# A long convolution by a two-stage Fourier transform: K's buffer as pairs of channels, and the product written into it

## The chip, the cores and the metric

The kernel runs on one core of one Trainium2 chip. The metric is the device time of one execution in microseconds. Before the change it is 544.58 us, the median of three runs (544.21 to 545.67). The engines are named as in the profile: PE is TensorE (PEld its weight loads, PEq its sequencer), DVE is VectorE, ACT is ScalarE, POOL is GpSimd, SP is SyncE, which issues nearly all DMAs.

## The reference

All data are float32. There are 2048 positions and 640 channels.

```
xn = layernorm(u)                                   # over the 640 channels
A  = -exp(log_A_real) + 1j*A_imag                   # 640 x 128 states
C  = (C_real + 1j*C_imag) * dt[:, None]
K  = 2 * einsum("dn,dnl->dl", C, exp(A*dt*l)).real  # one kernel of 2048 taps per channel
s  = irfft(rfft(xn, 4096) * rfft(K, 4096))[:2048] + xn * D_skip
g  = silu(xn + y)         # y: a gated feed-forward (640 -> 1728 -> 640) for the 8 positions
                          # with the highest xn @ w_r, zero elsewhere
out = u + s * g
```

So each channel is convolved with its own kernel of 2048 taps, and the gate is the silu of the normalized input, with 8 of the 2048 positions put through a feed-forward first.

## The kernel before, in words

**Tiling.** The 640 channels are seen as 4 blocks of 160 (the index d), the 2048 positions as 32 x 64. The large tile `g_all` is [128, 64, 2, 160]: partitions are (block, coarse position), then the fine position b, a real or imaginary plane, and 160 channel columns g, of which 32 neighbours make a batch. Seen as `gm` it is [128, 128 columns m, 160 channels g]. There are 5 batches (lines 25 to 29), each of 32 columns g, worked in groups of four: 40 groups.

**The steps of a batch.**

- K is generated for each group of four (`kernel`, line 819): POOL builds magnitudes by doubling (L829 to L836, tiles ma and mb), TensorE makes angles (L845), ACT takes their sine (L854), DVE multiplies (L856 to L867, tiles ta and tb), TensorE contracts over the states (L878), ACT copies the result into a buffer kb (L884; a ring of 5), and D_skip is added to its first tap (L885).
- First stage of the transform (`stage1`, line 897): K from kb gives a PSUM tile, which is copied into `fk` (L889 to L892), [128, 32 channels, 128 columns], channel by channel. For the input it is L906, copied back into `gm` (L908).
- Second stage (`transform`, line 913), for each kp from 0 to 7: a table `mt` of 4 x 128 columns is loaded; `dft` (L928) multiplies it with four columns of K (moving operand `k2`, from `fk`) and with four columns of the input (moving operand `u2`, from `gm`). In both, column 32 d + 4 kp + e belongs to kp. The moving operand runs over d and over the 32 channels.
- The complex product. K's result is copied to `kr` (L975), halves are swapped by DMAs into `ki` and `kr` (L976, L977), DVE forms `xa` (L989) and the main product (L992), which is written into `gm` over the input's columns (`u4`). `xa` has its halves swapped by DMAs into `xb` (L1007), and POOL adds it to `gm` (L1009; recorded as L392, since `tt` is a helper).
- In the last batch (QUICK) the input's transform is done early and copied into `gm` (L940 to L945), and for seven of the kp K's transform is made twice with its halves exchanged, in half-width matmuls (L958), so that no swap of K is needed.
- The inverse, four channels at a time (L1012 to L1022): the stationary operand is `gm[:, :, h + e]`, one channel's 128 columns with a step of 160 words; the moving operand is a constant. The result is copied into the same channels of `g_all` (L1020; recorded as L389, since `copy` is a helper), reading PSUM straight through and writing with a step of 160 words.
- The tail (line 1026) does the last inverse stage and the gate for the first three batches (L1047, L1054) and for the last two (L1118, L1124), adds the input and stores the output.

**What orders the work.** Every step is a task with the engines it can run on, a cost in us, what it reads and writes, and slots of rings of buffers. `Plan.order` simulates the engines and takes, on each engine, the ready task with the highest priority: the longest path behind it plus a weight from the table BIAS for its kind. PT is what a change of ACT's table set counts in that. The instructions are then issued in that order on every engine and on SP's queue. The task names that matter here are `s1k` and `s1ke` (first stage of K and its copy), `s2k`, `s2q`, `s2u` (second stages), `x1`, `xa`, `xadd` (the product), `inv` and `inve`.

**Who holds fk.** The first stage of the next batch's K may write `fk` as soon as the eight second-stage tasks of K of the batch before have read it (L889, key `fkfree` of the batch; L1010). The inverse of that batch reads `gm` and doesn't concern `fk`. Before the batches, `fk` serves as scratch (line 1146).

The lines that the steps of the prediction name:

```
copy(e, fk[:, q:q + 4].rearrange("p g m -> p (g m)"), p.t)                     # L891
k2 = fk[:, :ng].rearrange("p g (d k) -> p k d g", k=32)                        # L917
T.matmul(p.t[:, n * e:n * e + n], m.t[:, e], f[:, 4 * kp + e], start=True, stop=True)   # L930
T.matmul(p.t[:, 128 * e:128 * e + 128], gm[:, :, h + e], c[:, C_D:C_D + 128], start=True, stop=True)   # L1017
```

Of the kernel before, what the change touches and what calls it, by code (L numbers as in the profile page):

```python
# [21 lines left out]

L, D, N, FF, NSEL = 2048, 640, 128, 1728, 8
# [9 lines left out]
STEP = 7.3  # L33
# [5 lines left out]
PT = 45.962  # L39
BIAS = {  # L40
    "": -1188.3, "K": 3796.4, "arg": 1046.0, "evk": -8566.5, "exp": 2553.4, "ff": 15766.9, "inv": -8312.6,
    "inve": -8085.8, "kb": 907.3, "kswap": -0.0, "ln": 1669.4, "load": 11542.5, "mags": -1264.8, "mt": 4371.9,
# [23 lines left out]
def shape_constants():  # L66
# [25 lines left out]
    m[0, :, :, 1], m[1, :, :, 1] = np.sin(ph), np.cos(ph)  # L92
    l = 64 * a[None] + bm[:, None]
# [240 lines left out]
def kernel(ctx: ExitStack, tc: tile.TileContext, xq, xp, xr, par, ldtp, dsk, wr, wg, wu, wd,  # L334
# [19 lines left out]
    ring("kb", 5, [128, 4, 64], "fft")  # L354
# [14 lines left out]
    fk = k.tile([128, NG, 128], F32, name="fk")  # L369
    fuf = fk.rearrange("p g m -> p (g m)")  # L370
# [303 lines left out]
    def router():  # L674
        p = Slot("f")
        for j in range(5):
# [10 lines left out]
            on("PE", 1.52, mm, ["xn", ("wx", j)], [("rt", j)] + ([p] if j else []), [] if j else [p], mac=.853)  # L687
# [131 lines left out]
    def kernel(gg):  # L819
# [69 lines left out]
        on("PE", .9, lambda: stage1(p.t, lambda e: kb.t[:, e]), [kb, ("fkfree", batch(gg)), "c"], new=[p],  # L889
           kind="s1k", mac=.853)  # L890
        P.add(EVAC, lambda e: copy(e, fk[:, q:q + 4].rearrange("p g m -> p (g m)"), p.t),  # L891
# [21 lines left out]
    def transform(bi):  # L913
# [3 lines left out]
        k2 = fk[:, :ng].rearrange("p g (d k) -> p k d g", k=32)  # L917
        u2 = gm[:, :, g0:g0 + ng].rearrange("p (d k) g -> p k d g", k=32)
        vw = lambda t: t.rearrange("p (k d g) -> p k d g", k=4, d=4)
# [8 lines left out]
        def dft(p, f, m, kp):  # L928
            for e in range(4):
                T.matmul(p.t[:, n * e:n * e + n], m.t[:, e], f[:, 4 * kp + e], start=True, stop=True)  # L930
# [7 lines left out]
        if quick:  # L938

            for kp in range(8):  # L940
                m, pu, u4 = load_m(kp), Slot("f"), u2[:, 4 * kp:4 * kp + 4]
# [4 lines left out]
        for kp in range(8):  # L946
            m, xa = load_m(kp, [("U", bi, q) for q in range(8) if quick]), Slot("xa")
            kdep = [m] + [("fk", 4 * gg - g0) for gg in gs]
            u4 = u2[:, 4 * kp:4 * kp + 4]

            if quick and kp in QTWICE:
                pk = Slot("pr")

                def twice(pk=pk, m=m, kp=kp):
                    for h in range(2):
                        for e in range(4):
                            for half in range(2):
                                T.matmul(pk.t[64 * half:64 * half + 64, 1 - h, n * e:n * e + n],  # L958
                                         m.t[:, e, 64 - 64 * h:128 - 64 * h], k2[:, 4 * kp + e], start=True, stop=True,
                                         tile_position=(0, 64 * half))  # L960

                on("PE", 3.9, twice, kdep, [("S2K", bi, kp)], [pk], kind="s2q", mac=1.707)
# [6 lines left out]
                on("DVE", .6, lambda u4=u4, pk=pk: V.tensor_tensor(u4, u4, vw(pk.t[:, 0, :nn]), op=OP.mult),  # L969
                   [pk], [("X", bi, kp)], kind="x1")  # L970
            else:
                pk, krk, kik, pu = Slot("f"), Slot("kr"), Slot("ki"), Slot("f")
                on("PE", 1.78, lambda pk=pk, m=m, kp=kp: dft(pk, k2, m, kp), kdep, [("S2K", bi, kp)], [pk, krk],
# [8 lines left out]
                if quick:  # L982
# [3 lines left out]
                    on("DVE", .6, lambda u4=u4, krk=krk: V.tensor_tensor(u4, u4, vw(krk.t[:, :nn]), op=OP.mult),  # L986
# [215 lines left out]
```

## Time and profile before

| | us |
|---|---|
| median of three runs | 544.58 |
| the profiled execution | 540.41 |
| its span, first to last instruction | 538.6 |
| from the start to the first second-stage matmul of K | 139.3 |
| first inverse | 219.4 |
| last K product (L878) begins | 416.0 |
| last batch's K transform (L958) begins | 449.4 |

The granted clock of TensorE was 0.993 on average. A float32 matmul shows as two records in the trace, so that a call of `dft` (four matmuls) is eight records. The durations of single TensorE records overlap: the mean ns of one is its latency, and the price in a stream comes from the start and the end of an unbroken run. A group's idle time names what ended it; for an engine that isn't the bottleneck it costs nothing. DMA share is the mean busy share of the core's 16 DMA engines.

### The profile page before, as it was taken

How to read it: one execution, taken by the hardware profiler on the slowest of the kernel's cores; microseconds unless marked ns; L12 is line 12 of the kernel's file. 1: busy time of each engine (PE TensorE's matmuls, PEld its weight loads, DVE VectorE, ACT ScalarE, POOL GpSimd, SP SyncE). 2: the span in 40 equal slices, each digit the busy share in tenths (PEclk: the TensorE clock that was granted, in tenths of full speed). 3: DMA queues.
4: the chain of work that ended last, by engine and by line, in shares of the span. 5: the costliest groups of instructions: out<-in, count | busy, mean ns of one | idle time of the engine just before them, and what ended most of it. 6: DMA issues, size and time to landing. Idle time of an engine off the chain costs nothing.

```text
span 538.6 us, 16912 instructions
## 1 busy us (share of the span) xinstructions
PE 486.8 (90%) x6871; PEld 391.5 (73%) x6871; DVE 381.7 (71%) x801; ACT 291.6 (54%) x437; POOL 304.5 (57%) x706
## 2 busy tenths in 40 slices
PE   1039999999998899999999999999999999999994
PEld 1014977656665568888889878888888998866984
DVE  6999099774579846999877999778834133578245
ACT  2009587677734248955677657866645542332420
POOL 7250459973759586898968998958942900000000
PEclk9999999999998999989999999999999999999999
DMA  8909502544789962246642656115675187798956
GB/s 255 311 1 276 138 28 77 167 135 146 194 205 202 219 163 62 71 99 173 185 114 49 160 129 179 41 35 156 158 219 144 52 214 201 203 261 266 258 162 192
DMA packets 91126, 84.84 MB, mean 158 GB/s; under 512 B 41384, under 2 KB 65640, under 8 KB 91048
## 3 DMA queue, kind: packets, MB, share of 16 engines
q1 hardware_dynamic: 90792, 83.71, 57.2%
q8 instruction: 54, 0.88, 0.7%
q14 instruction: 24, 0.20, 0.1%
q0 software_dynamic: 256, 0.04, 0.0%
HBM read 50.02 MB, written 10.51 MB: 112 GB/s over the span
## 4 chain that ended last, share of the span: by engine, by line
PE 60%; DVE 14%; DMA 12%; POOL 5%; SPq 5%; issue 3%; ACT 1%; DVEq 0%; POOLq 0%; ACTq 0%
PE f L901 13%; PE f L930 11%; PE f L1017 9%; PE pr L845 5%; PE f L878 5%; DMA wflat<-wd 5%; PE f L404 3%; PE f L767 3%; PE f L685 2%; PE f L1047 2%; DMA xb<-xa 2%; PE pr L958 2%; SPq L419 2%; POOL mb L834 2%; DMA g_all<-xq 1%
## 5 line engine op out<-in xcount | busy, mean ns | idle before, releaser
L834 POOL TENSOR_TENSOR mb<-mb,et 128x32 f32<-128x32 f32 (+4 forms) x200 | 107.9, 540 | 0.0
L854 ACT ACTIVATE pr<-pr 128x1024 f32<-128x1024 f32 x80 | 81.2, 1020 | 34.7 <-PE pr L845 32.4
L389 ACT COPY g_all<-f 128x512 f32<-128x512 f32 x65 | 64.3, 1000 | 52.7 <-PE f L1017 35.9
L1017 PE MATMUL f<-c,g_all 128*128 128x128 f32 x320 | 75.1, 383 | 0.0
L1017 PEld LDWEIGHTS f<-c,g_all 128*128 128x128 f32 x320 | 72.6, 311 | 3.0 <-issue 0.9
L836 POOL TENSOR_TENSOR ma<-ma,et 128x16 f32<-128x16 f32 (+4 forms) x200 | 74.6, 373 | 0.0
L858 DVE TENSOR_TENSOR tb<-pr,mb 128x512 f32<-128x512 f32 x80 | 54.5, 681 | 18.6 <-PE f L878 15.3
L930 PE MATMUL f<-fk,mt 128*128 128x128 f32 x264 | 63.1, 398 | 1.2 <-DVE fk L389 1.2
L930 PEld LDWEIGHTS f<-fk,mt 128*128 128x128 f32 x264 | 52.8, 206 | 9.0 <-DVE fk L389 1.4
L856 DVE TENSOR_TENSOR ta<-pr,ma 128x512 f32<-128x512 f32 x80 | 54.3, 682 | 6.8 <-ACT pr L854 3.2
L901 PEld LDWEIGHTS f<-c,g_all 128*64 128x64 f32 x640 | 49.7, 250 | 11.1 <-issue 3.6
L392 POOL TENSOR_TENSOR g_all<-g_all,xb 128x512 f32<-128x512 f32 x32 | 41.1, 1287 | 26.8 <-DMA xb<-xa 11.9
L901 PE MATMUL f<-c,g_all 128*64 128x128 f32 x640 | 55.0, 319 | 0.1
L845 PE MATMUL pr<-pos,st 128*128 128x512 f16 x160 | 48.1, 386 | 2.1 <-DVE sv L440 1.2
L878 PE MATMUL f<-tb,ta 128*32 128x64 f32 x2560 | 47.3, 223 | 0.0
L878 PEld LDWEIGHTS f<-tb,ta 128*32 128x32 f32 x2560 | 40.5, 111 | 9.1 <-issue 5.1
L930 PE MATMUL f<-g_all,mt 128*128 128x128 f32 x320 | 43.9, 284 | 0.9 <-DMA mt<-cm 0.6
L930 PEld LDWEIGHTS f<-g_all,mt 128*128 128x128 f32 x320 | 40.3, 196 | 5.9 <-issue 3.1
L901 PE MATMUL f<-c,kb 128*64 128x128 f32 x640 | 40.5, 276 | 0.0
L901 PEld LDWEIGHTS f<-c,kb 128*64 128x64 f32 x640 | 34.7, 137 | 6.9 <-issue 2.8
L389 DVE COPY g_all<-f 128x512 f32<-128x512 f32 x23 | 24.3, 1057 | 17.2 <-PE f L901 14.5
L1072 POOL MEMSET wflat<- 128x2048 f32 x1 | 1.8, 1808 | 58.3 <-DVE g_all L1054 58.3
(155 smaller groups left out, 807.2 us busy)
## 6 DMA issues: line engine op xcount, KB each, us to landing
mt<-cm SPq DMA_DIRECT2D x48, 256.0 KB
xb<-xa SPq DMA_DIRECT2D x78, 128.0 KB
ki<-kr SPq DMA_DIRECT2D x66, 128.0 KB
g_all<-xq SPq DMA_DIRECT2D x8, 640.0 KB
xg_d<-g_all SPq DMA_DIRECT2D x16, 320.0 KB
wflat<-wg SPq DMA_DIRECT2D x10, 432.0 KB
wflat<-wu SPq DMA_DIRECT2D x10, 432.0 KB
wflat<-wd SPq DMA_DIRECT2D x16, 270.0 KB
```

What stands on the lines that cost most here:

```text
L389: {"ACT": S.copy, "DVE": V.tensor_copy, "POOL": G.tensor_copy}[e](out, in_)
L392: {"DVE": V, "POOL": G}[e].tensor_tensor(out, a, b, op=op)
L834: G.tensor_tensor(b[:, :, :, w:2 * w], b[:, :, :, :w], e[:, q].unsqueeze(2).unsqueeze(3).broadcast_to([128, 16, 2, w]), op=OP.mult)
L836: G.tensor_tensor(a[:, :, w:2 * w], a[:, :, :w], e[:, 6 + q].unsqueeze(2).broadcast_to([128, 16, w]), op=OP.mult)
L845: T.matmul(o.t[:, h], st.t[:, 2 * (gg % 8) + h], pos[:, 512 * f:512 * f + 512], start=True, stop=True)
L854: on("ACT", .96, lambda src=src: S.activation(src.t, src.t, AF.Sin, scale=-TWO_PI), [], [src], table="TS", kind="sin")
L856: on("DVE", .6, lambda i=i, src=src: V.tensor_tensor(half(ta.t[:, i]), side(src, 0), half(ma.t), op=OP.mult), [src, ma] + ([] if i else [t ...
L858: on("DVE", .6, lambda i=i, src=src: V.tensor_tensor(half(tb.t[:, i, :, 0]), side(src, 1)[:, :, :, ::-1], half(mb.t[:, :, 1]), op=OP.mult) ...
L878: T.matmul(o[32 * d4:32 * d4 + 32, dl, :], ta.t[:, i, cc, :], tb.t[:, i, cc].rearrange("p h j -> p (h j)"), start=(i == 0), stop=(i == 1), ...
L901: T.matmul(p[64 * ri:64 * ri + 64, 128 * e:128 * e + 128], src(e), c[:, C_W + 128 * ri:C_W + 128 * ri + 128], start=True, stop=True, tile_ ...
L930: T.matmul(p.t[:, n * e:n * e + n], m.t[:, e], f[:, 4 * kp + e], start=True, stop=True)
L1017: T.matmul(p.t[:, 128 * e:128 * e + 128], gm[:, :, h + e], c[:, C_D:C_D + 128], start=True, stop=True)
```

## The change

`fk` becomes [128, 16 pairs, 128 columns, 2]: the two channels of a pair are neighbours, then the columns, then the pairs. Columns are dealt to kp in another way: column 32 d + 8 i + kp belongs to kp, so that the sixteen columns of one kp have a constant step of 8; the table `cm` has its rows permuted to match. The transforms write their PSUM tile in the order (d, i, channel), in four runs of 32 columns per matmul.

The main product and the addition of `xb` now write into `fk` (`z4`), over those columns of K that this kp's transform has read; `gm` keeps the input's values until the inverse's copy. The inverse takes its stationary operand from `fk`: one channel's 128 columns with a step of two words. Its copy reads PSUM with a step of 128 words and writes four neighbouring words at a time.

The place of four channels in `fk` now becomes free when their inverse has read it, so `fkfree` is kept for each group of four instead of for the batch. The ring kb grows from 5 to 8 buffers. The copy of K into `fk` writes every second word.

The planner's costs of `s2k` and `inv` become 0.95 us and that of `s2q` 2.0, and the router's 2.6, and PT and all weights in BIAS are others, so that the order of issue on every engine can differ.

```
-    ring("kb", 5, [128, 4, 64], "fft")
+    ring("kb", 8, [128, 4, 64], "fft")
...
-    fk = k.tile([128, NG, 128], F32, name="fk")
+    fk = k.tile([128, NG // 2, 128, 2], F32, name="fk")
...
+    m = m[:, :, (np.arange(8)[:, None] + 8 * np.arange(4)).reshape(-1)]
...
-        on("PE", .9, lambda: stage1(p.t, lambda e: kb.t[:, e]), [kb, ("fkfree", batch(gg)), "c"], new=[p],
+        on("PE", .9, lambda: stage1(p.t, lambda e: kb.t[:, e]), [kb, ("fkfree", q), "c"], new=[p],
            kind="s1k", mac=.853)
-        P.add(EVAC, lambda e: copy(e, fk[:, q:q + 4].rearrange("p g m -> p (g m)"), p.t),
+        P.add(EVAC, lambda e: copy(e, fk[:, q // 2:q // 2 + 2].rearrange("p h m r -> p h r m"),
+                                   p.t.rearrange("p (h r m) -> p h r m", h=2, r=2)),
...
+        k2 = fk.rearrange("p h (d i k) r -> p i k d h r", d=4, k=8)
+        u2 = gm[:, :, g0:g0 + ng].rearrange("p (d i k) g -> p i k d g", d=4, k=8)
+        vw = lambda t: t.rearrange("p (x g) -> p x g", x=16)
+        vz = lambda t: t.rearrange("p (x h r) -> p x h r", x=16, r=2)
+        vc = lambda t, e: t.rearrange("p (d i g) -> p i d g", d=4, i=4)[:, e]
+        vu = lambda t: t.rearrange("p x (h r) -> p x h r", r=2)
+        in_u = lambda kp: gm[:, kp::8, g0:g0 + ng]
+        in_z = lambda kp: fk[:, :, kp::8].rearrange("p h x r -> p x h r")
...
-                T.matmul(p.t[:, n * e:n * e + n], m.t[:, e], f[:, 4 * kp + e], start=True, stop=True)
+                T.matmul(vc(p.t[:, :nn], e), m.t[:, e], f[:, e, kp], start=True, stop=True)
...
-                    on("DVE", .6, lambda u4=u4, pu=pu, krk=krk: V.tensor_tensor(
-                        u4, vw(pu.t[:, :nn]), vw(krk.t[:, :nn]), op=OP.mult), [pu, krk], [("X", bi, kp)], kind="x1")
+                    on("DVE", .6, lambda z4=z4, pu=pu, krk=krk: V.tensor_tensor(
+                        z4, vz(pu.t[:, :nn]), vz(krk.t[:, :nn]), op=OP.mult), [pu, krk, ("S2K", bi, kp)], [("X", bi, kp)],
+                       kind="x1")
...
-                     lambda e, u4=u4, xb=xb: tt(e, u4, u4, vw(xb.t[:, :nn]), OP.add), [xb], [("X", bi, kp)], kind="xadd")
-        P.join([("fkfree", bi + 1)], [("S2K", bi, kp) for kp in range(8)])
+                     lambda e, z4=z4, xb=xb: tt(e, z4, z4, vz(xb.t[:, :nn]), OP.add), [xb], [("X", bi, kp)], kind="xadd")
...
-                    T.matmul(p.t[:, 128 * e:128 * e + 128], gm[:, :, h + e], c[:, C_D:C_D + 128], start=True, stop=True)
...
-            P.chain(("i", gg % 8), on("PE", 1.77, inv, [("Xall", bi), "c"], new=[p], kind="inv", mac=.853), 8 * STEP)
-            P.add(EVAC_COL, lambda e, p=p, h=h: copy(
-                e, g_all[:, :, :, h:h + 4].rearrange("p b r g -> p g b r"),
-                p.t.rearrange("p (g b r) -> p g b r", g=4, b=64)), [p], [("y", bi, gg)], kind="inve")
+                    T.matmul(p.t[:, 128 * e:128 * e + 128], fk[:, (q + e) // 2, :, e % 2], c[:, C_D:C_D + 128],
+                             start=True, stop=True)
+
+            P.chain(("i", gg % 8), on("PE", .95, inv, [("Xall", bi), "c"], [("fkfree", h - g0)], [p], kind="inv", mac=.853),
+                    8 * STEP)
+            P.add(EVAC_COL, lambda e, p=p, h=h: copy(e, gm[:, :, h:h + 4], p.t.rearrange("p (g m) -> p m g", g=4)),
+                  [p] + [("U", bi, kp) for kp in range(8)], [("y", bi, gg)], kind="inve")
...
-    P.join([("fkfree", 0)], ["diag", "ones", "m2"] + [("sts", b) for b in range(0, NB, 4)])
+    for q in range(0, NG, 4):
+        P.join([("fkfree", q)], ["diag", "ones", "m2"] + [("sts", b) for b in range(0, NB, 4)])
```

The same change of target is made in the last batch's two forms of the product.

More of the change, by code (lines that the diff above doesn't have):

```diff
@@ L38 @@
 QTWICE = (1, 2, 3, 4, 5, 6, 7)
-PT = 45.962
+PT = 51.488
 BIAS = {
-    "": -1188.3, "K": 3796.4, "arg": 1046.0, "evk": -8566.5, "exp": 2553.4, "ff": 15766.9, "inv": -8312.6,
-    "inve": -8085.8, "kb": 907.3, "kswap": -0.0, "ln": 1669.4, "load": 11542.5, "mags": -1264.8, "mt": 4371.9,
[6 rows of a table removed]
+    "": -182.6, "K": 20620.6, "arg": 3785.6, "evk": -1312.8, "exp": 2366.8, "ff": -119.1, "inv": 21575.7,
+    "inve": 7516.6, "kb": 285.9, "kswap": -6679.6, "ln": -1.4, "load": -1205.7, "mags": 9237.9, "mt": 1730.4,
[5 rows of a table added]
+    307.9, "xadd": 15271.2, "xq": -6876.5, "xswap": -876.9,
 }
@@ L368 @@
     gm = g_all.rearrange("p b r g -> p (b r) g")
-    fk = k.tile([128, NG, 128], F32, name="fk")
-    fuf = fk.rearrange("p g m -> p (g m)")
+    fk = k.tile([128, NG // 2, 128, 2], F32, name="fk")
+    fuf = fk.rearrange("p h m r -> p (h m r)")
     c = k.tile([128, C_END], F32, name="c")
@@ L686, in mm @@
                              start=(j == 0 and i < 4), stop=(j == 4 and i > 27), tile_position=(0, t))
-            on("PE", 1.52, mm, ["xn", ("wx", j)], [("rt", j)] + ([p] if j else []), [] if j else [p], mac=.853)
+            on("PE", 2.6, mm, ["xn", ("wx", j)], [("rt", j)] + ([p] if j else []), [] if j else [p], mac=.853)
         r4 = wflat[:, L:L + 64]
@@ L940, in transform @@
             for kp in range(8):
-                m, pu, u4 = load_m(kp), Slot("f"), u2[:, 4 * kp:4 * kp + 4]
+                m, pu, u4 = load_m(kp), Slot("f"), in_u(kp)
                 P.chain(("u", kp), on("PE", .95, lambda pu=pu, m=m, kp=kp: dft(pu, u2, m, kp), [m] + udep, [("U", bi, kp)],
@@ L948, in transform @@
             kdep = [m] + [("fk", 4 * gg - g0) for gg in gs]
-            u4 = u2[:, 4 * kp:4 * kp + 4]
+            u4, z4 = in_u(kp), in_z(kp)
             if quick and kp in QTWICE:
@@ L957, in twice @@
                             for half in range(2):
-                                T.matmul(pk.t[64 * half:64 * half + 64, 1 - h, n * e:n * e + n],
-                                         m.t[:, e, 64 - 64 * h:128 - 64 * h], k2[:, 4 * kp + e], start=True, stop=True,
+                                T.matmul(vc(pk.t[64 * half:64 * half + 64, 1 - h, :nn], e),
+                                         m.t[:, e, 64 - 64 * h:128 - 64 * h], k2[:, e, kp], start=True, stop=True,
                                          tile_position=(0, 64 * half))
-                on("PE", 3.9, twice, kdep, [("S2K", bi, kp)], [pk], kind="s2q", mac=1.707)
+                on("PE", 2.0, twice, kdep, [("S2K", bi, kp)], [pk], kind="s2q", mac=1.707)
                 on("ACT", .57, lambda pk=pk: S.activation(pk.t[:, 1, :nn], pk.t[:, 1, :nn], AF.Copy,
@@ L968, in transform @@
                    [pk, ("sK", bi, kp), ("X", bi, kp)], new=[xa], kind="xa")
-                on("DVE", .6, lambda u4=u4, pk=pk: V.tensor_tensor(u4, u4, vw(pk.t[:, 0, :nn]), op=OP.mult),
+                on("DVE", .6, lambda u4=u4, z4=z4, pk=pk: V.tensor_tensor(z4, vu(u4), vz(pk.t[:, 0, :nn]), op=OP.mult),
                    [pk], [("X", bi, kp)], kind="x1")
@@ L985, in transform @@
                         vw(xa.t[:, :nn]), u4, vw(kik.t[:, :nn]), op=OP.mult), [kik, ("X", bi, kp)], new=[xa], kind="xa")
-                    on("DVE", .6, lambda u4=u4, krk=krk: V.tensor_tensor(u4, u4, vw(krk.t[:, :nn]), op=OP.mult),
-                       [krk], [("X", bi, kp)], kind="x1")
+                    on("DVE", .6, lambda u4=u4, z4=z4, krk=krk: V.tensor_tensor(z4, vu(u4), vz(krk.t[:, :nn]), op=OP.mult),
+                       [krk, ("S2K", bi, kp)], [("X", bi, kp)], kind="x1")
                 else:
@@ L1002, in transform @@
                 on("PE", .9, turn, [xa, "c"], new=[ps2], kind="xq")
-                on("DVE", .6, lambda u4=u4, ps2=ps2: V.tensor_tensor(u4, u4, vw(ps2.t[:, :nn]), op=OP.add), [ps2],
+                on("DVE", .6, lambda z4=z4, ps2=ps2: V.tensor_tensor(z4, z4, vz(ps2.t[:, :nn]), op=OP.add), [ps2],
                    [("X", bi, kp)], kind="xq")
```

7 lines of the change are left out of this document (2 added, 5 removed), and 11 rows, old and new, of the table BIAS.

## The prediction

> **What bounds the kernel now.** The page comes first: the share of each engine, and the chain of work that ended last.
>
> ```profile
> span 538.6 us, 16912 instructions
> PE 486.8 (90%) x6871; PEld 391.5 (73%) x6871; DVE 381.7 (71%) x801; ACT 291.6 (54%) x437; POOL 304.5 (57%) x706
> PE 60%; DVE 14%; DMA 12%; POOL 5%; SPq 5%; issue 3%; ACT 1%; DVEq 0%; POOLq 0%; ACTq 0%
> ```
>
> TensorE is busy 90% of the span and is 60% of the chain, but DVE, the DMAs and POOL hold 31% of it. A cut in TensorE work is therefore not worth the same everywhere, and the second view is the busy time by stretch (columns: length, then PE, PE weight loads, DVE, ACT and POOL busy with their instruction counts, granted clock, DMA share, GB/s). I cut at 220 us (the first inverse), at 350 (near the end of the dense K generation) and at 449 (the last batch's K transform).
>
> ```profile
> 68.00:220.00 152.00, 145.84 (x2144) 102.11 (x2143) 115.02 (x233) 96.66 (x135) 106.66 (x258) 0.99 0.54 142
> 220.00:350.00 130.00, 126.89 (x1822) 110.35 (x1821) 117.51 (x221) 90.32 (x136) 114.94 (x287) 0.99 0.48 124
> 350.00:449.00 99.00, 98.09 (x1302) 88.56 (x1302) 52.26 (x84) 54.41 (x75) 53.11 (x104) 1.00 0.53 144
> 449.00:538.60 89.60, 80.38 (x1196) 66.29 (x1192) 48.86 (x87) 24.36 (x39) 2.83 (x2) 1.00 0.78 220
> ```
>
> From 68 us on TensorE hardly rests. Yet from 220 to 350 DVE is at 90% and POOL at 88% as well, so there three engines end within 12 us of each other. From 350 to 449 TensorE is alone (99%; DVE and POOL 53 and 54%). From 449 on the DMA engines are at 0.78.
>
> The third view is the groups by shape. It says which TensorE instructions are dear (count, then busy us and the mean ns of one).
>
> ```profile
> L1017 PE MATMUL f<-c,g_all 128*128 128x128 f32 x320 | 75.1, 383 | 0.0
> L1017 PEld LDWEIGHTS f<-c,g_all 128*128 128x128 f32 x320 | 72.6, 311 | 3.0 <-issue 0.9 <-DVE g_all L1003 0.2 <-ACT fk L389 0.2
> L930 PE MATMUL f<-fk,mt 128*128 128x128 f32 x264 | 63.1, 398 | 1.2 <-DVE fk L389 1.2
> L930 PE MATMUL f<-g_all,mt 128*128 128x128 f32 x320 | 43.9, 284 | 0.9 <-DMA mt<-cm 0.6 <-ACT g_all L389 0.3
> L930 PEld LDWEIGHTS f<-g_all,mt 128*128 128x128 f32 x320 | 40.3, 196 | 5.9 <-issue 3.1 <-ACT fk L389 0.9 <-ACT g_all L389 0.4
> L958 PE MATMUL pr<-fk,mt 128*64 128x128 f32 x224 | 29.6, 438 | 1.6 <-DVE g_all L969 1.6
> ```
>
> All rows of L930 and L1017 have one shape, 128 rows by 128 columns in float32. What differs is how the operand lies. In g_all 32 channels lie side by side (L930, 284 ns). In fk the next channel is 128 words on (L930 with fk, 398 ns). The inverse's stationary operand steps over 160 words (L1017: its weight load takes 311 ns against 196). These durations overlap, so the price of one comes from unbroken runs in the timeline of TensorE (start, length, line, count):
>
> ```profile
> 288.63 5.49 PE L930 MATMUL f<-fk,mt 128*128 128x128 f32 x24
> 402.69 4.94 PE L930 MATMUL f<-g_all,mt 128*128 128x128 f32 x40 [0.27 <-DMA mt<-cm]
> 409.56 4.59 PE L901 MATMUL f<-c,kb 128*64 128x128 f32 x80
> 423.63 5.33 PE L1017 MATMUL f<-c,g_all 128*128 128x128 f32 x24
> 460.45 7.65 PE L958 MATMUL pr<-fk,mt 128*64 128x128 f32 x64
> ```
>
> Per record that is 229 ns with fk, 124 ns with g_all, 57 ns for a half-width one with dense operands, 222 ns for the inverse, 120 ns for the half-width one with fk.
>
> **The change, part by part: the cheaper operands.** In the new fk two channels lie side by side and the next pair 256 words on. So K's moving operand comes in runs of two words. I take the dense price for it: 229 - 124 = 105 ns saved on each of 264 records, 27.7 us. The half-width ones (L958) go from 120 to 57 ns: 224 x 63 = 14.1 us. The inverse's stationary operand now steps over two words instead of 160. Again I take the dense price, 222 - 124 = 98 ns on 320 records, 31.4 us. Together 73 us. The bounds are the dense price and today's: no row shows runs of two words or a step of two, so either saving can also be nil; I stand nearer the dense rows, because pairs halve the jumps and a step of 8 bytes lies far nearer to 4 than to 640.
>
> [...]
>
> **Where these savings count.** The records by stretch (PE's count is the first in brackets; tile fk, then line 1017):
>
> ```profile
> 68.00:220.00 152.00, 15.60 (x64) 12.54 (x64) 0.70 (x1) 8.33 (x14) 0.99 0.54 142
> 220.00:350.00 130.00, 30.31 (x128) 25.90 (x128) 2.72 (x4) 7.11 (x12) 0.99 0.48 124
> 350.00:449.00 99.00, 17.17 (x72) 14.37 (x72) 0.00 (x0) 5.22 (x9) 1.00 0.53 144
> 220.00:350.00 130.00, 29.47 (x126) 28.43 (x125) 0.99 0.48 124
> 350.00:449.00 99.00, 30.10 (x128) 28.96 (x128) 1.00 0.53 144
> 449.00:538.60 89.60, 14.92 (x64) 14.37 (x64) 1.00 0.78 220
> ```
>
> - 68 to 220: 64 x 105 = 6.7 us. TensorE is not busy for 6.2 us of the stretch, so others already hold part of it; I count 4.
> - 220 to 350: 128 x 105 + 126 x 98 = 25.8 us. DVE still has its 117.5 us; at 96% busy the stretch would be 122.4 long. I count 8: DVE and POOL are next in line and keep the other 18.
> - 350 to 449: 72 x 105 + 128 x 98 = 20.1 us, and nothing else is near. I count 20.
> - 449 to the end: 14.1 + 64 x 98 = 20.4 us. The same bytes at a DMA share of 0.90 instead of 0.78 need 89.6 x 0.78 / 0.90 = 77.7 us. I count 11.
>
> The sum is 43 us. The profiled execution took 540.4 us, its span 538.6 and 1.8 around it; it lies 4.2 us below the median of the runs, 544.6. So 540.4 - 43 = 497.4 profiled, and 502 as a median.
>
> **The other edits.**
>
> ```profile
> L389 ACT COPY fk<-f 128x512 f32<-128x512 f32 x35 | 20.7, 594 | 6.8 <-PE f L901 6.7
> L389 DVE COPY fk<-f 128x512 f32<-128x512 f32 x5 | 3.4, 684 | 0.1
> L389 DVE COPY g_all<-f 128x512 f32<-128x512 f32 x23 | 24.3, 1057 | 17.2 <-PE f L901 14.5
> L992 DVE TENSOR_TENSOR g_all<-f,kr 128x512 f32<-128x512 f32 x32 | 21.5, 678 | 0.0
> L389 ACT COPY g_all<-f x65: 586/1052/1144, 71.8 to 515.7; 128x512 f32<-128x512 f32 x65
> L392 POOL TENSOR_TENSOR g_all<-g_all,xb 128x512 f32<-128x512 f32 x32 | 41.1, 1287 | 26.8 <-DMA xb<-xa 11.9 <-PE pr L845 6.7 <-DVE tb L867 4.6
> L834 POOL TENSOR_TENSOR mb<-mb,et 128x32 f32<-128x32 f32 x40 | 10.9, 273 | 0.0
> L836 POOL TENSOR_TENSOR ma<-ma,et 128x32 f32<-128x32 f32 x40 | 10.4, 261 | 0.0
> ```
>
> The copy of K into fk (40 of them) now writes every second word: on ACT between 594 ns and the 1052 ns of a copy into columns of g_all. I take 594; at worst it is 40 x 0.46 = 18 us of ACT, which is busy 90 of 130 us in its fullest stretch, and one copy of delay in each of four batches, 2 us. The product's write in pairs (40 on DVE) costs 678 ns as now up to 678 + (1057 - 684) = 1051: nil taken, at worst 24 x 0.37 = 9 us on DVE where it bounds. The inverse's copy reads PSUM with a step of 128 words and writes four words together: between 586 and 1052 + 466 = 1518 ns; I take today's 1052, since one hop replaces another. POOL's addition (1287 ns) over pairs: 32 elements in single words take POOL 273 ns, in pairs 261, so hops are nearly free there; nil taken, twice the time as the upper end. The transforms' output in PSUM goes in four runs of 32 columns instead of one of 128, three jumps per matmul; nil. The bytes of the tables and of the swaps through SP's queue stay.
>
> Added is a wait. The first stage of K for four channels now waits for the inverse of the four channels that held their place, where it waited for the last K transform only. It stands on TensorE's queue; behind it wait the angles and products of the next K groups, and the whole next transform. Eight kb buffers instead of five let K generation run on meanwhile. All queues are issued in another order; the rows can't price that. The four stretches hold 19 us in which TensorE isn't busy, so I allow 10 either way.
>
> **Rivals.** The stages of the loop that the new wait closes, from the first K transform of a batch to its last addition:
>
> ```profile
> 228.66 2.00 PE L930 MATMUL f<-fk,mt 128*128 128x128 f32 x8 [1.24 <-DVE fk L389]
> 281.01 1.29 POOL L392 TENSOR_TENSOR g_all<-g_all,xb 128x512 f32<-128x512 f32 x1 [2.96 <-PE pr L845]
> 343.56 1.27 POOL L392 TENSOR_TENSOR g_all<-g_all,xb 128x512 f32<-128x512 f32 x1
> 355.24 2.00 PE L930 MATMUL f<-fk,mt 128*128 128x128 f32 x8
> 410.27 2.53 POOL L392 TENSOR_TENSOR g_all<-g_all,xb 128x512 f32<-128x512 f32 x2 [0.89 <-DMA xb<-xa]
> 449.40 7.74 PE L958 MATMUL pr<-fk,mt 128*64 128x128 f32 x64
> ```
>
> With 288.63 from above the stages last 53.6, 56.2 and 57.6 us. Today the next one starts 6.3 and 10.4 us after the last addition (36.6 before the last batch, with the tail's work in between), its K already in fk. With the change 64 inverse records (7.9 us), 128 first-stage records (7.3) and a copy (0.6) come between: 15.8.
>
> 1. *The forecast, 502.* Each stage loses its own 64 x 105 = 6.7 us, so 49.1 on average. Started 4 us earlier, the last batch's K transform comes at 224.7 + 3 x (49.1 + 15.8) = 419, 30 us before today's, which agrees with 4 + 8 + 20. Chance 0.50, own range 485 to 518.
> 2. *The loop bounds.* Swaps, additions and DVE, not TensorE, set the stage, and it stays as long. Then the K transforms start at 282.3 + 15.8 = 298.1, + 56.2 + 15.8 = 370.1, + 57.6 + 15.8 = 443.5, which is 5.9 us before today's; with the first stretch's 4 and the tail's 11 that is 21 us: 524. For it: POOL and DVE at 88 and 90%. Against it: TensorE was full in every stage. Chance 0.17.
> 3. *Only the moving operand gains.* A weight load may pay for every word that doesn't lie next to the last, whatever the step; then the inverse stays at 222 ns and its load at 311. By stretch I count 4, 6 (TensorE keeps 12 us more there), 7.6 and 9, so 27 us, 518. Against it: none of the rows has a step below 640 bytes. [...] Chance 0.12.
> 4. *All of it comes through*, the new order filling DVE and POOL evenly: 544.6 - 73 = 472. Against it: the DMAs of the tail. Chance 0.11.
> 5. *Slower: POOL's addition over pairs takes twice its time*, 2.6 us. It lies in the loop eight times a batch: three stages of 10.3 us more against the second rival's 21 us, 31 - 21 = 10: 555. It decides from 21 / 24 = 0.9 us more per addition. Against it: 273 and 261 ns above. Chance 0.05.
> 6. *The pairs do nothing for TensorE.* The loop then holds 14.2 + 7.3 + 0.6 = 22.1 us between stages, and the last K transform starts at 462.5: 13 later, 558. Chance 0.03.
>
> **The numbers.** The likeliest gives 502. Faster by over 0.3% (1.6 us, about what a measurement of this kernel can tell from no change): 0.50 + 0.17 + 0.12 + 0.11 = 0.90. Slower: 0.08. The 0.02 left lies between. A range of 476 to 530 takes in the first three cases and the upper half of the fourth; it leaves out the slower ones.
>
> **What would show it.** Right: the fk transform and the inverse near 280 ns each with a weight load under 200, TensorE's busy sum near 415 us, its share below 90%, DVE above 76%, the last K transform near 419 us. The second rival shows as waits of TensorE for the copy into fk, and stages still 54 to 58 us; the third as L1017's weight load still near 311; the fifth as additions over 2.2 us. The forecast is wrong if TensorE's sum falls by 73 us and the span by less than 20, or if POOL's or DVE's sums grow by over 15 us.

## The result, and the profile after

The changed kernel takes 525.6 us, the median of four runs (521.7 to 528.6), against 545.1 for four runs of the kernel before: a ratio of 0.963, interval 0.956 to 0.971. That is 19.6 us faster, inside the range, and less than half of the 42.6 us that were forecast. The profiled execution took 528.6 us, the slowest of the four; the one before took 540.4, less than any of its four, so that the spans of the two profiles differ by 11.8 us only. The times below are medians over all runs, while the ratios leave out one disturbed run in each of three kernels.

The page of the changed kernel, the same three lines as before:

```profile
span 526.8 us, 16914 instructions
...
PE 433.9 (82%) x6895; PEld 344.3 (65%) x6895; DVE 405.5 (77%) x816; ACT 272.1 (52%) x426; POOL 305.2 (58%) x702
...
PE 34%; DVE 28%; DMA 20%; SPq 8%; issue 4%; POOL 3%; ACT 2%; DVEq 0%; POOLq 0%; ACTq 0%
```

TensorE's sum fell by 52.9 us, the span by 11.8. So 41.1 us of new idle time on TensorE took the place of work. Its share of the chain fell from 60% to 34%; DVE, the DMAs and SP's queue have taken it over.

The groups by shape (count, then busy us and the mean ns of one, then idle time and its releasers):

```profile
L1028 PE MATMUL f<-c,fk 128*128 128x128 f32 x320 | 40.5, 290 | 1.8 <-POOL fk L395 1.6 <-DVE fk L395 0.2
...
L1028 PEld LDWEIGHTS f<-c,fk 128*128 128x128 f32 x320 | 39.6, 203 | 3.5 <-POOL fk L395 2.4 <-issue 0.9
...
L941 PE MATMUL f<-fk,mt 128*128 128x128 f32 x264 | 34.3, 275 | 1.4 <-DMA mt<-cm 0.8 <-ACT kb L887 0.5
...
L969 PE MATMUL pr<-fk,mt 128*64 128x128 f32 x224 | 17.3, 313 | 0.0
...
L1003 DVE TENSOR_TENSOR fk<-f,kr 128x512 f32<-128x512 f32 x32 | 21.7, 681 | 7.1 <-PE f L941 4.5 <-DMA kr<-kr 2.5
...
L395 POOL TENSOR_TENSOR fk<-fk,xb 128x512 f32<-128x512 f32 x32 | 41.9, 1312 | 42.3 <-DMA xb<-xa 36.7 <-ACT kr L986 4.3 <-DVE ta L859 1.0
```

The inverse and K's transform have the dense price, 284 ns with `gm` before, or near it. The inverse's records went from 383 to 290 ns and its weight load from 311 to 203, K's transform from 398 to 275, the half-width one from 438 to 313. In busy time that is 34.6, 28.8 and 12.3 us, together 75.7. The edits that were taken as free are free: 681 ns for the product (678 before), 1312 for POOL's addition (1287). But POOL now waits 36.7 us for the swapped `xb` where it waited 11.9.

Where the idle time lies is seen when both spans are cut at the starts of K's transforms. Busy time by stretch (length, PE, weight loads, DVE, ACT, POOL, granted clock, DMA share, GB/s). The kernel before:

```profile
139.30:228.70 89.40, 83.24 (x1087) 60.17 (x1085) 68.81 (x132) 50.53 (x78) 67.73 (x166) 0.98 0.63 156
228.70:288.60 59.90, 59.58 (x872) 51.80 (x873) 53.43 (x104) 39.39 (x59) 50.33 (x118) 0.97 0.51 129
288.60:355.20 66.60, 65.06 (x961) 56.31 (x961) 60.27 (x106) 45.72 (x65) 60.00 (x155) 1.00 0.44 112
355.20:449.40 94.20, 93.29 (x1194) 84.45 (x1192) 47.38 (x78) 51.55 (x70) 49.30 (x94) 1.00 0.56 153
449.40:538.60 89.20, 79.98 (x1186) 66.01 (x1184) 48.86 (x87) 23.96 (x38) 2.83 (x2) 1.00 0.78 219
```

The changed kernel, cut at the same events:

```profile
138.90:214.50 75.60, 67.21 (x1050) 54.74 (x1048) 60.83 (x120) 48.84 (x72) 57.73 (x137) 0.98 0.56 150
214.50:292.70 78.20, 65.00 (x959) 47.28 (x956) 60.22 (x117) 40.91 (x63) 54.67 (x136) 0.93 0.70 183
292.70:366.70 74.00, 64.62 (x1019) 50.39 (x1018) 57.30 (x101) 40.00 (x58) 57.23 (x134) 0.95 0.62 151
366.70:455.90 89.20, 81.95 (x1406) 72.43 (x1405) 57.71 (x93) 47.24 (x71) 46.50 (x94) 1.00 0.76 207
455.90:526.80 70.90, 57.69 (x1038) 51.39 (x1036) 43.45 (x76) 23.74 (x40) 1.80 (x1) 0.96 0.80 218
```

The middle three rows are the loop, three cycles: each from one batch's K transform to the next one's. Before, TensorE was idle for 0.3, 1.5 and 0.9 us of them; now for 13.2, 9.4 and 7.2. These 27.1 us are most of the 41.1. In the first two, 78.2 and 74.0 us long, no engine is above 88%: DVE has 77%, POOL 70 and 77%. The gain stands in the first row (13.8 us) and the last (18.3); the loop gives 20.7 of it back (78.2 + 74.0 + 89.2 against 59.9 + 66.6 + 94.2). The 0.4 us left is the start before the first row.

The timeline of the changed kernel (start, length) shows the turn from one batch to the next: the last addition of a batch, the inverse, the first stage of the next K, K's transform. The additions are on POOL, the rest on TensorE.

```profile
273.21 1.29 POOL L395 TENSOR_TENSOR fk<-fk,xb 128x512 f32<-128x512 f32 x1
...
276.68 7.80 PE L1028 MATMUL f<-c,fk 128*128 128x128 f32 x64
284.42 7.21 PE L905 MATMUL f<-c,kb 128*64 128x128 f32 x128
...
292.67 1.50 PE L941 MATMUL f<-fk,mt 128*128 128x128 f32 x12
...
348.59 1.31 POOL L395 TENSOR_TENSOR fk<-fk,xb 128x512 f32<-128x512 f32 x1
...
366.75 2.86 PE L941 MATMUL f<-fk,mt 128*128 128x128 f32 x24
...
434.94 2.52 POOL L395 TENSOR_TENSOR fk<-fk,xb 128x512 f32<-128x512 f32 x2 [9.42 <-DMA xb<-xa]
...
455.89 1.16 PE L941 MATMUL f<-fk,mt 128*128 128x128 f32 x8
...
456.98 4.87 PE L969 MATMUL pr<-fk,mt 128*64 128x128 f32 x64
```

The 64 inverse records take 7.80 us, 122 ns each (222 before), and 24 of K's transform 2.86 us, 119 each (229 before). The half-width ones, in the last row, take 76 ns each: less than the 120 before, but not the 57 that were taken. The turn lasts 292.7 - 274.5 = 18.2 us, where 15.8 were worked out. But the stages themselves, from K's transform to the last addition, last 274.5 - 214.5 = 60.0, 57.2 and 70.8 us; before it was 53.6, 56.2 and 57.6, and 49.1 was forecast.

Busy time in the same two turns, then in the stages ahead of them (columns as above):

```profile
274.50:292.70 18.20, 18.20 (x241) 15.92 (x232) 12.77 (x30) 14.54 (x29) 10.85 (x34) 0.97 0.20 47
349.90:366.70 16.80, 16.80 (x262) 15.87 (x261) 7.27 (x12) 13.77 (x25) 12.29 (x31) 1.00 0.20 58
```

```profile
214.50:274.50 60.00, 46.80 (x730) 31.37 (x730) 47.45 (x87) 26.38 (x35) 43.82 (x103) 0.93 0.85 224
292.70:349.90 57.20, 47.82 (x759) 34.52 (x757) 50.03 (x90) 26.23 (x34) 44.94 (x104) 0.94 0.74 179
```

In the turn TensorE is full and the DMA engines are at 0.20. In the stage it is the other way round: the DMAs at 0.85 and 0.74 (0.55 and 0.52 in the same stages before), and TensorE idle for 13.2 and 9.4 us, which is all the idle time of its cycles. So the kernel now alternates between a stretch that belongs to TensorE and one that belongs to DMAs, DVE and POOL.

What the stage waits for: the chain that ended last, a piece of stage 1 of the changed kernel (start, length, what).

```profile
223.03 5.01 DMA wflat<-wu
...
237.58 6.39 DMA xb<-xa
...
248.51 4.23 DMA xb<-xa
...
255.64 4.92 DMA wflat<-wu
...
266.51 5.77 DMA wflat<-wd
```

`wu` and `wd` are weights of the feed-forward, which before was multiplied between 90 and 202 us, ahead of the first inverse, and is now between 175 and 330, in the stages of the loop. TensorE waits for these weights: between 214 and 330 us its weight loads wait 7.3 us for `wu` (L770) and 4.0 us for `wd` (L798). The swaps into `xb`, which the stage needs, are issued on the same queue of SP.

### The profile page after: what moved, and what is told of

The parts are those of the page before. It is cut to its first block, busy times and chain, and to the rows that moved or that the text cites. A ratio compares the mean times of both kernels' runs of the same rounds, so it can differ in the third digit from the quotient of the medians.

```text
span 526.8 us, 16914 instructions
## 1 busy us (share of the span) xinstructions
PE 433.9 (82%) x6895; PEld 344.3 (65%) x6895; DVE 405.5 (77%) x816; ACT 272.1 (52%) x426; POOL 305.2 (58%) x702
## 4 chain that ended last, share of the span: by engine, by line
PE 34%; DVE 28%; DMA 20%; SPq 8%; issue 4%; POOL 3%; ACT 2%; DVEq 0%; POOLq 0%; ACTq 0%
PE f L905 9%; DMA xb<-xa 7%; PE f L1028 6%; DVE tb L861 4%; DVE ta L859 4%; PE f L941 4%; PE f L881 3%; SPq L422 3%; PE pr L848 3%; DVE tb L870 2%; DMA kr<-xp 2%; PE f L1059 2%; DVE g_all L446 2%; DVE tb L868 2%; DMA wflat<-wu 2%
## 5 line engine op out<-in xcount | busy, mean ns | idle before, releaser
L837 POOL TENSOR_TENSOR mb<-mb,et 128x32 f32<-128x32 f32 (+4 forms) x200 | 111.5, 557 | 0.0
L839 POOL TENSOR_TENSOR ma<-ma,et 128x16 f32<-128x16 f32 (+4 forms) x200 | 78.0, 390 | 0.0
L861 DVE TENSOR_TENSOR tb<-pr,mb 128x512 f32<-128x512 f32 x80 | 59.0, 737 | 15.8 <-PE f L881 8.7
L395 POOL TENSOR_TENSOR fk<-fk,xb 128x512 f32<-128x512 f32 x32 | 41.9, 1312 | 42.3 <-DMA xb<-xa 36.7
L859 DVE TENSOR_TENSOR ta<-pr,ma 128x512 f32<-128x512 f32 x80 | 60.2, 753 | 2.8 <-ACT pr L857 1.8
L392 ACT COPY g_all<-f 128x512 f32<-128x512 f32 x57 | 47.0, 832 | 28.7 <-PE f L1028 13.7
L1028 PE MATMUL f<-c,fk 128*128 128x128 f32 x320 | 40.5, 290 | 1.8 <-POOL fk L395 1.6
L1028 PEld LDWEIGHTS f<-c,fk 128*128 128x128 f32 x320 | 39.6, 203 | 3.5 <-POOL fk L395 2.4
L887 ACT COPY kb<-f 128x256 f32<-128x256 f32 x40 | 14.8, 371 | 51.2 <-PE f L881 49.2
L941 PEld LDWEIGHTS f<-fk,mt 128*128 128x128 f32 x264 | 32.4, 189 | 6.6 <-ACT kr L986 1.4
```

Source lines behind the costliest of these rows:

```text
L392: {"ACT": S.copy, "DVE": V.tensor_copy, "POOL": G.tensor_copy}[e](out, in_)
L395: {"DVE": V, "POOL": G}[e].tensor_tensor(out, a, b, op=op)
L837: G.tensor_tensor(b[:, :, :, w:2 * w], b[:, :, :, :w], e[:, q].unsqueeze(2).unsqueeze(3).broadcast_to([128, 16, 2, w]), op=OP.mult)
L839: G.tensor_tensor(a[:, :, w:2 * w], a[:, :, :w], e[:, 6 + q].unsqueeze(2).broadcast_to([128, 16, w]), op=OP.mult)
L859: on("DVE", .6, lambda i=i, src=src: V.tensor_tensor(half(ta.t[:, i]), side(src, 0), half(ma.t), op=OP.mult), [src, ma] + ([] if i else [t ...
L861: on("DVE", .6, lambda i=i, src=src: V.tensor_tensor(half(tb.t[:, i, :, 0]), side(src, 1)[:, :, :, ::-1], half(mb.t[:, :, 1]), op=OP.mult) ...
```

## The experiments

Two explanations were on the table from this profile. *The loop*: the new wait makes inverse, first stage and transform follow each other, so that what ran beside the stages is now outside them, whatever else is done. *The moved loads*: the new order of issue has put the feed-forward's weights into the stages, and it is these that lengthen them. A third, that a single dear edit does it (a copy, an addition), had little left after the groups above.

**The feed-forward's loads cut**, in the changed kernel, the order untouched: 34 of its 36 weight loads carry a sixteenth of their bytes, so that its numbers are left out.

```
-                    o[:FJ, :, :320], wdv[:, 2 * i[1]:2 * i[1] + 2, h, 320 * i[0]:320 * i[0] + 320]), dep, [key], up=10.0)
+                    o[:FJ, :, :20], wdv[:, 2 * i[1]:2 * i[1] + 2, h, 320 * i[0]:320 * i[0] + 20]), dep, [key], up=10.0)
...
-                P.dma(4.4e5, lambda e: nc.sync.dma_start(o, w[128 * i:128 * i + 128, 2 * FC * h:2 * FC * h + 2 * FC].rearrange(
-                    "p (h f) -> p h f", h=2)), dep, [key], up=10.0)
+                m = FC if n < len(ring) else 27
+                P.dma(4.4e5, lambda e: nc.sync.dma_start(
+                    o[:, :, :m], w[128 * i:128 * i + 128, 2 * FC * h:2 * FC * h + 2 * FC].rearrange(
+                        "p (h f) -> p h f", h=2)[:, :, :m]), dep, [key], up=10.0)
```

> The changed kernel with its order of issue untouched; of the experts' 36 weight loads all but the first two carry a sixteenth of their bytes (the feed-forward's numbers are left out by that). Two theories. The loop: the place in fk is held from K's first stage to the inverse, so that generation of the next K stops when its eight buffers are full, and a stage (first K transform to last addition) is as long as its own chain of swaps and additions. The moved loads: the new order puts the experts' loads into the first two stages, where they stand between the swaps on SP's queue and TensorE's queue waits for them. Moved loads expects stages of about 50 us in place of 62.2 and 57.7 (batches 1 and 2), the last batch's K transform near 436 instead of 455.9, and 505 us in place of 525.6. The loop alone expects stages of at least 56 and 520 us or more.

Measured: 508.7 us, ratio 0.924 (0.917 to 0.932), and the last batch's K transform at 437.9, near the 505 and 436 expected of the moved loads. Its busy time in the first two cycles of the loop:

```profile
209.30:276.70 67.40, 60.36 (x958) 43.34 (x955) 58.90 (x117) 40.78 (x63) 55.65 (x137) 1.00 0.52 121
276.70:346.40 69.70, 64.82 (x1020) 51.11 (x1018) 55.87 (x101) 40.06 (x58) 56.49 (x133) 0.95 0.49 124
```

The cycles shrink from 78.2 and 74.0 to 67.4 and 69.7 us, their stages from 60.0 and 57.2 to 50.2 and 52.4 (the expectation's 62.2 and 57.7 run to the first inverse), near the 49.1 of the forecast. The DMA issues of the two kernels show how; the last column is the median us from issue to landing. The changed kernel:

```profile
xb<-xa SPq DMA_DIRECT2D x78, 128.0 KB, 4.8
```

With the loads cut:

```profile
xb<-xa SPq DMA_DIRECT2D x78, 128.0 KB, 2.9
```

The loads are a cause, then. Whether they are the change's own needs the same cut in the kernel before.

**The same cut in the kernel before** (the same edit).

> The control for the first experiment: the kernel before the change, its order untouched, with the same 34 of the experts' weight loads cut to a sixteenth of their bytes (the feed-forward's numbers are left out by that). If the loads cost the old order as much as the new one, about 20 us (4% of the time), then moving them isn't where the change's gain went. If it is the new order that puts them in a bad place, the old kernel gains clearly less, 8 us (1.5%) or less. The old order has them in the stage of batch 0, which is 69 us long, so I expect something between: 10 to 15 us.

Measured: 540.7 us, ratio 0.987 (0.983 to 0.990). The loads cost the old order 1.4%, some 7 us, less than the 10 to 15 expected. They cost the changed kernel 1 - 0.9243 / 0.9635 = 4.1%, some 21 us. So about 14 us are loads that the old order hid and the new one doesn't.

**No loop.** K in pairs as in the change, but the product goes back into `gm`, and `fkfree` is kept per batch as before. The inverse's stationary operand comes from a constant table with a step of two words (but for the first matmul of each batch), so that it has the cheap price without the data; the order is planned anew.

```
-        on("PE", .9, lambda: stage1(p.t, lambda e: kb.t[:, e]), [kb, ("fkfree", q), "c"], new=[p],
+        on("PE", .9, lambda: stage1(p.t, lambda e: kb.t[:, e]), [kb, ("fkfree", batch(gg)), "c"], new=[p],
...
-        in_z = lambda kp: fk[:, :, kp::8].rearrange("p h x r -> p x h r")
+        in_z = in_u
...
-                    T.matmul(p.t[:, 128 * e:128 * e + 128], fk[:, (q + e) // 2, :, e % 2], c[:, C_D:C_D + 128],
-                             start=True, stop=True)
+                    one = gm[:, :, h + e] if not begun else c[:, C_W:C_W + 256:2]
+                    T.matmul(p.t[:, 128 * e:128 * e + 128], one, c[:, C_D:C_D + 128], start=True, stop=True)
```

> K's buffer in pairs as in the change, but the product goes back into g_all and the place in fk is free after the last K transform, as before the change. The inverse takes a constant of step two words as its stationary operand, except in the first matmul of each batch, so that it is as cheap as in the change and still waits for the batch; what is left out is the true operand of the other inverses. The order of issue is found anew for this kernel. The loop expects all of TensorE's 73 us to come nearer: the last batch's K transform before 430 (455.9 with the change), stages free to overlap, and below 500 us. Moved loads expects no such gain, since the experts' loads still lie among the stages: 515 us or more.

Measured: 504.1 us, ratio 0.921 (0.915 to 0.926). The expectation of under 500 us was missed by 4; the last batch's K transform, expected before 430, comes at 423.2. The ratio of the forecast was 502 / 544.6 = 0.922. The timeline of TensorE in this kernel before its last addition of batch 1, which starts at 282.57:

```profile
260.27 2.87 PE L904 MATMUL f<-c,kb 128*64 128x128 f32 x32
...
265.70 2.84 PE L904 MATMUL f<-c,kb 128*64 128x128 f32 x48
...
272.94 1.09 PE L904 MATMUL f<-c,kb 128*64 128x128 f32 x16
```

The next batch's first stage of K starts at 260, 22 us ahead of that addition; in the changed kernel it starts 10 us behind it (284.42 against 274.50). That is what the loop forbids. It costs 0.9635 - 0.9206 = 0.043 of 545 us, some 23 us.

**No loop, and the loads cut** (both edits).

> The kernel without the loop (second experiment: the inverse takes a constant for most matmuls), its order untouched, with the experts' loads cut in the same way (the feed-forward's numbers are left out too). If loop and loads are two separate costs, their gains add: 0.92 of the kernel before becomes about 0.88. If they are one cost seen twice (the loads only hurt because the loop leaves no slack), it stays above 0.91.

Measured: 486.6 us, ratio 0.889 (0.886 to 0.893), against 0.88 expected from adding the two. So they are two causes, and without either the time is back at the forecast's (0.924 and 0.921 beside its 0.922); without both it is shorter, since the forecast let only 43 of the 73 us through. With the loads cut in both kernels the loop costs 0.9243 - 0.8892 = 0.035, some 19 us, so that most of its 23 us don't come from where the loads lie. And here the loads cost 1 - 0.8892 / 0.9206 = 3.4%, without any loop. Not the loop makes the loads dear, then. That a TensorE with 57 us less work covers less of them, or that these orders put them late, fits this, but no run separates the two.

**The wait alone**, on the old operands: the kernel before, with `fkfree` per four channels released by the inverse, and eight kb buffers; the order is planned anew.

```
-        on("PE", .9, lambda: stage1(p.t, lambda e: kb.t[:, e]), [kb, ("fkfree", batch(gg)), "c"], new=[p],
+        on("PE", .9, lambda: stage1(p.t, lambda e: kb.t[:, e]), [kb, ("fkfree", q), "c"], new=[p],
...
-            P.chain(("i", gg % 8), on("PE", 1.77, inv, [("Xall", bi), "c"], new=[p], kind="inv", mac=.853), 8 * STEP)
+            P.chain(("i", gg % 8), on("PE", 1.77, inv, [("Xall", bi), "c"], [("fkfree", h - g0)], [p], kind="inv", mac=.853), 8 * STEP)
```

> The wait alone: the kernel before the change with its old operands, in which the first stage of K for four channels now waits for the inverse of the four channels in that place, and with eight kb buffers. Nothing is left out; the order of issue is found anew for it. If the wait has no price, 548 us as before (ratio 1.00). If the loop is what took the change's gain, each of three batches pays an inverse, a first stage and a gap that nothing covers: 20 to 35 us more, a ratio of 1.04 to 1.06.

Measured: 585.0 us, ratio 1.063 (1.055 to 1.071), just above the 1.04 to 1.06 expected of the loop. The forecast's sixth rival, pairs that do nothing for TensorE, had given 558. In the timeline inverse and first stage alternate, four channels by four:

```profile
296.93 2.02 PE L1016 MATMUL f<-c,g_all 128*128 128x128 f32 x8
298.88 1.09 PE L901 MATMUL f<-c,kb 128*64 128x128 f32 x16
299.91 0.60 PE L845 MATMUL pr<-pos,st 128*128 128x512 f16 x2
300.35 1.82 PE L1016 MATMUL f<-c,g_all 128*128 128x128 f32 x8
```

All 64 inverse records and 128 first-stage ones stand between two stages here too; at the old prices a turn takes 25 to 37 us, where the sixth rival had 22.1.

**Pairs alone.** K in pairs, product and inverse in `gm` at today's 222 ns, `fkfree` per batch; eight kb buffers and the change's copy of the inverse are kept, and the order is planned anew. It computes the whole reference.

```
+    fk = k.tile([128, NG // 2, 128, 2], F32, name="fk")
+        k2 = fk.rearrange("p h (d i k) r -> p i k d h r", d=4, k=8)
+        in_z = in_u
```

> One part of the change alone: K's buffer in pairs with the new dealing of columns, eight kb buffers, but the product stays in g_all and the inverse reads it there with its step of 160 words; the inverse's copy is the changed one. Nothing is left out, and the order of issue is found anew. TensorE keeps 31 of the 73 us. The loop expects that this does as well as the whole change or better, 505 to 525 us, since the 31 us are paid back by the overlap of batches. If the loop costs nothing, 42 of 73 parts of the whole gain of 20 us are left: about 533.

Measured: 523.4 us, ratio 0.955 (0.949 to 0.961). So half of the change does as well as the whole: to save the inverse's 35 us of TensorE's work one has to take the loop, and the loop costs as much as that saving brings.

**The copy of the input's first stage turned**, in the changed kernel: it reads PSUM with a step of 128 words and writes four neighbouring words, as the change does for the inverse.

```
-            e, gm[:, :, g0:g0 + 4].rearrange("p m g -> p g m"), p.t.rearrange("p (g m) -> p m g", g=4)),
+            e, gm[:, :, g0:g0 + 4], p.t.rearrange("p (g m) -> p m g", g=4)),
```

> The changed kernel with one more copy turned round in the same way as the change turned the inverse's: the copy of the input's first stage reads PSUM with a step of 128 words and writes four neighbouring words, in place of reading straight and writing with a step of 160 words. Order of issue untouched; nothing left out. In the changed kernel's profile the inverse's turned copy takes 586 ns on ACT and 692 on DVE, the unturned one 1067 and 1036. So the 40 copies should fall to those 586 and 692, which frees about 18 us of ACT and DVE. These copies are seldom what TensorE waits for: 0 to 4 us of the time.

Measured: 527.5 us, ratio 0.965 (0.960 to 0.970), beside the change's 0.963. ACT's copies into `g_all` fell from 47.0 to 33.1 us (57 of them, 832 to 586 ns in the mean), and nothing came of it. ACT, at 52%, isn't what the loop waits for.

**Planned anew with measured costs.** Three kernels, pairs alone, the whole change and the kernel before, with both copies turned and the planner's costs set from the traces; the orders are found anew by the same search.

```
-    DMA_RATE, DMA_LAT, DMA_ISSUE = 360e3, (0.0, 0.65, 0.95), 0.06
+    DMA_RATE, DMA_LAT, DMA_ISSUE = 250e3, (0.0, 0.65, 1.6), 0.06
...
+            eng = [(e, x * self.CAL.get((e, kind), self.CAL.get(e, 1.0))) for e, x in eng]
```

> The pairs alone (third experiment), with both copies into g_all turned round, and the order found anew with a planner whose costs are scaled to the profiles (TensorE, POOL and the DMAs dearer). Nothing is left out. It has no loop and 31 us more TensorE work than the change. The loop expects it ahead of the changed kernel and of the next experiment: 500 to 515 us. If the order is what matters and not the loop, the next one is the faster.

> The whole change, with both copies turned round and the order found anew by the same planner with the same effort. The loop expects it to stay behind the pairs alone by 10 us or more, though TensorE has 31 us less to do: 515 to 530. If the recorded order was at fault, it comes to about 502.

> The control for the two others: the kernel before the change with both copies turned round and the order found anew in the same way. It shows what order and copies are worth without pairs: between 525 and 550 us. What lies between it and the pairs alone is then the price of K's moving operand, 42 us of TensorE work at most.

Measured on one chip: pairs alone 521.3 us, ratio 0.946 (0.941 to 0.951); the whole change 530.4, 0.965 (0.959 to 0.972); the kernel before 538.2, 0.980 (0.974 to 0.987). The pairs alone missed their upper end by 6 us and the whole change its own by 0.4, but the pairs alone beat both other kernels. The kernel before gains 2.0% by order and copies alone, so that the pairs themselves, with eight kb buffers, are worth 3.5%, some 19 us. The whole change gains nothing from a new order, which speaks against bad luck with the one that it has; the loop stays.

## Why the prediction was wrong

**Right: the operands, but for one.** 73 us were worked out, and the busy time of the three groups fell by 75.7. Per record of an unbroken run the inverse and K's transform saved the 98 and 105 ns that were taken, or a little more (100 and 110). The half-width one was mis-sized: from 120 to 76 ns it saved 224 x 44 = 9.9 us, where 14.1 were taken; why it stays above the 57 of dense operands was not tried. The weight load at a step of 8 bytes takes 203 ns beside 196 dense. No row before the result showed runs of two words or a step of two: the dense price for both was the author's estimate, from the dense rows, and the runs bear it out at full width. The third rival, a weight load that stays at 311, is refuted by the 203.

**Right: the free edits.** The product (681 ns beside 678), POOL's addition (1312 beside 1287) and the output in runs of 32 columns (the input's transform still takes 284 ns) cost next to nothing; the fifth rival is refuted. The copy of K takes 638 ns on ACT in the median where 594 was taken and 1052 was the bound. The inverse's copy was taken too dear, see below.

**Wrong: "Each stage loses its own 64 x 105 = 6.7 us, so 49.1 on average."** This is the step that failed, and with it the last K transform at 419: it came at 456. The turn around it was worked out well, at 15.8 us against 16.8 to 18.4. The cycle was to be 49.1 + 15.8 = 64.9 us and was 78.2, 74.0 and 89.2. Three things were missing in it:

1. *The loads.* The three stages that the chain of 64.9 us goes by held no feed-forward in the old order, which had it between 90 and 202 us; in the new one two of them do. With the loads cut they last 50.2 and 52.4. "All queues are issued in another order; the rows can't price that", with 10 us either way, was too little: the experiments give 14.
2. *The turn takes its work out of TensorE's stage, but nobody else's.* A stage of 49.1 supposed that TensorE sets its length. With inverse and first stage in the turn TensorE has only 46.8 and 47.8 us left in the stage, and the swaps, products and additions of one batch, and the K generation of the next, go on for longer. With the loads cut DVE is busy for 91% of both stages (45.9 of 50.2 us and 47.9 of 52.4) and POOL for 88 and 84%, TensorE for 86 and 91%. The swaps hardly use the turn: the DMAs are at 0.20 there. In the first turn K's products stand too (the last of a batch ends at 275.3, the next one's first starts at 294.6; without the loop at 280.3 and 285.1); in the second one is made at 357.7, and there the kernel without the loop has a gap too (335.8 to 361.8). The experiments without the loop price this at 19 to 23 us; which of DVE, POOL and the swaps sets the stage then was not tried.
3. *The last cycle.* The chain of 64.9 us took no account of the work of the tail and the later input, of which the prediction itself said that it lies ahead of the last batch. This cycle held 93.3 us of TensorE's work before; less the 20.1 that were to be saved it leaves 73, more than the whole cycle was to last. In the changed kernel it holds 82, and TensorE is busy for 92% of it. These groups of it show why:

```profile
L1059 PE MATMUL f<-g_all,wflat 64*64 64x96 f32 x320 | 15.2, 245 | 1.5 <-DMA wflat<-cw 1.5
L905 PE MATMUL f<-c,g_all 128*64 128x128 f32 x160 | 13.5, 319 | 0.0
```

The kernel before had 160 of the first kind in this cycle (7.5 us) and 34 of the second (3.2 us); 64 of its 128 inverse records have left it (7.8 us). 73 + 7.7 + 10.3 - 7.8 = 83, near the 82. That work was moved in from the tail and from the batches ahead. It is paid back where it came from: the tail is 18.3 us shorter, where 11 was forecast, and the first row above 13.8, where 4 was. So the gains outside the loop were larger than forecast by 17 us, and the loop lost 21 where it should have gained 26.

Two ways of counting had agreed on 30 us by the last K transform, the stretches (4 + 8 + 20) and the chain of stages. They agreed on the sum alone: by the stretches the first two cycles were to be 59 us on average and the last 74, by the chain 64.9 each.

**The second rival**, the loop that bounds, gave 524, and 525.6 was measured; that they lie so close is partly luck. It was right in its core (the stage doesn't shrink with TensorE's work), but not in its numbers: its last K transform was to come at 439.5 (443.5 less the first stretch's 4) and came 16 later, the tail was 7 us shorter than it said, and its 21 us were 11.8 between the profiles and 19.6 between the medians. Its sign, waits of TensorE for the copy into fk, didn't show: K's transform waited 1.4 us in all, for its table and for kb. It named swaps, additions and DVE as what sets the stage. In the stages DVE is at 79 and 87%, POOL at 73 and 79%, the DMAs at 0.85 and 0.74; of these the experiments have tested the DMAs alone.

**The tests that were set.** The first, "if TensorE's sum falls by 73 us and the span by less than 20", came true for the span (11.8) and, with 75.7, for the three groups; the whole sum fell by 52.9, to 433.9 where 415 was forecast. The warm-up matmuls went from 18.1 to 25.7 us and the router's from 13.0 to 17.9; and the rows of all TensorE's groups, which overlap in time, fell from 522 to 457 us, 12 more than the whole sum. The second, "if POOL's or DVE's sums grow by over 15 us", came true for DVE: 381.7 to 405.5 us, of which the products `ta` and `tb` are 10.4.

**What stays open.** The order of issue is another one in every kernel that was planned anew, so that the loop's price holds what the search found in either. A second buffer for K, which would open the loop with the true data, wasn't tried. In the kernel with the loads cut stage 3 still lasts 72 us; that the moved work sets it is read from the groups, and no run took that work out. DVE's products `ta` rose from 682 to 753 ns and `tb` from 681 to 737; why wasn't tried.

## What to carry to other kernels

When a buffer is handed on within a loop, don't take the cycle as the old stage less its savings plus the new steps: list for each cycle all the work of every engine that must lie in it, DMAs too, and ask what runs beside the new steps. When an order is planned anew, look where the loads of unrelated work have gone, and whether the engine that is to become faster was their cover. And price the parts of a change one by one: here the half without the new wait gives all of the gain.

## What the runs showed of the hardware

The copies of the changed kernel by destination (count, then the least, median and largest ns, first and last start):

```profile
L392 ACT COPY g_all<-f x57: 567/1004/1164, 113.2 to 502.7; 128x512 f32<-128x512 f32 x57
...
L392 DVE COPY g_all<-f x31: 684/692/1152, 115.0 to 500.8; 128x512 f32<-128x512 f32 x31
...
L392 ACT COPY fk<-f x31: 610/638/769, 66.6 to 454.5; 128x512 f32<-128x512 f32 x31
...
L392 DVE COPY fk<-f x9: 665/692/696, 77.4 to 450.2; 128x512 f32<-128x512 f32 x9
```

- The first two rows mix two patterns and eight copies of the last batch. The inverse's 40 copies, which read PSUM with a step of 512 bytes and write 16 bytes at a time, take 586 ns on ACT and 692 on DVE in the median; those that read PSUM straight and write single words with a step of 640 bytes take 1067 and 1036. The copies into `fk` of the kernel before, dense on both sides, took 587 and 692. So a hop of 512 bytes in the source with 16 bytes together in the destination takes no longer here than a dense copy. The prediction had 586 to 1518 ns for it and took 1052.
- Single words written 8 bytes apart take 692 ns on DVE in the median, as the dense copy did, and 638 on ACT, where the dense copy took 587.
- A half-width matmul (64 columns of weights) over pairs takes 76 ns per record in an unbroken run (64 in 4.87 us), one of K's first stage with dense operands 56 (128 in 7.21), though at full width pairs cost nothing (119 ns beside 124). Whether the pairs do it or the output in four runs was not tried.
- TensorE's granted clock was 0.93, 0.95 and 1.00 in the loop's three cycles, with 13.2, 9.4 and 7.2 us of idle time; with the loads cut it was 1.00 in the first with 7.0 idle and 0.95 in the second with 4.9. So idle time alone doesn't order it, and the cause was not tried.
